# A fused attention and feed-forward kernel: its prologue rebuilt (q loaded first, attention of the first chunk spread over all free PSUM banks, column means of w_out by an fp32 matmul, chunk 1's attention one step earlier and chunk 2's later)

## The chip, the cores and the metric

The kernel runs on one core of a Trainium2 chip. The metric is device time in microseconds (us), from the first to the last instruction of the launch as the runtime counts it; "span" is the same stretch as the profile shows it, about 2 us shorter. Engines are named as in the profile: PE is the matrix engine (PEld its weight loads), DVE the vector engine, ACT the scalar (activation) engine, POOL the GpSimd engine, SP the engine that here issues the output transfers (and three small loads at the start). "Clock" is the share of the full TensorE clock that was granted. Runs are marked fast or slow (over 1.5% above the fastest of the same kernel); only fast ones are compared.

## The reference

```python
def _attn_ref(q, k, v, g_norm):                       # (8 batches, 8 heads, 576, 64)
    kv = np.einsum('bhsd,bhse->bhde', k, v)           # linear attention: no softmax
    out = np.einsum('bhsd,bhde->bhse', q, kv)
    rms = np.sqrt(np.mean(out * out, axis=-1, keepdims=True) + 1e-06)
    return out / rms * g_norm

def _moe_ref(x, w_in, w_out, g_ln):                   # x (4608, 512), w_in (512, 1024)
    h = x @ w_in
    e = np.exp(h - np.max(h, axis=-1, keepdims=True))
    solu = h * (e / (np.sum(e, axis=-1, keepdims=True) + 1e-09))
    mu = np.mean(solu, axis=-1, keepdims=True)
    var = np.mean((solu - mu) ** 2, axis=-1, keepdims=True)
    return ((solu - mu) / np.sqrt(var + 1e-06) * g_ln) @ w_out
```

The attention output, with its heads side by side, is the x of the second function. Everything is float32 at the boundary.

## The kernel before

The 4608 tokens are worked on as nine chunks of 512: one for the first 512 tokens of each batch, and a ninth with the 8 x 64 that remain. A chunk passes through attention (kv, q transposed, o, and the root-mean-square over a head by a matmul with `head_mean`, called s), through eight steps h(c, 0..7) (each four matmuls, an exp on ACT, a product u on DVE, its square usq and a pair sum es on POOL), through statistics (sums, then a few tiny DVE operations), and through the output product.

The layer norm's subtraction of the mean is not done on the tokens. It is folded into the second weight: each row of `w_out * g_ln` has the mean over d_ff of its column taken off, once, in the prologue. So no output matmul may start before that mean is known and the weight is centred:

```python
    def w_out_scale(f, eng):
        eng.tensor_scalar_mul(out=w_out_g[:, f, :], in0=w_out_f[:, f, :], scalar1=g_ln_sb[:, f:f + 1])

    def w_out_mean():
        mean[0] = po.tile([128, d_model], FP32, name="mean_ps", tag="out")
        for f in range(NF):                       # NF = 8; col_mean is 1/1024 everywhere, BF16
            nc.tensor.matmul(mean[0][:, :], col_mean[:, :], w_out_g[:, f, :], start=(f == 0), stop=(f == NF - 1))

    def w_out_center(f):
        nc.vector.scalar_tensor_tensor(
            out=w_out_sb[:, f, :], in0=w_out_f[:, f, :], scalar=g_ln_sb[:, f:f + 1],
            in1=mean[0][:, :], op0=MUL, op1=SUB,
        )
```

The attention of a chunk, per pair of heads p, goes over three PSUM tiles of the pool `pat`:

```python
    def o_mm(c, p):
        ...
        t = pat.tile([128, 512], FP32, name="o_ps", tag="at")
        ... # one matmul kvbd x qT
        osq = work.tile([128, 512], BF16, name="osq")          # work has two buffers of a name
        nc.scalar.activation(out=osq[:, :], in_=t[:, :], func=AF.Square, bias=zero_t[:, :])

    def s_mm(c, p):
        t = pat.tile([128, 512], FP32, name="s_ps", tag="at")
        nc.tensor.matmul(t[:, :], head_mean[:, :], osq_sb.pop((c, p))[:, :], start=True, stop=True)
        ... # lss = Ln(t) and rst = Exp(-0.5 * lss) on ACT
        ... # x_sb = o_ps * g_rep * rst on DVE
```

A plan `at(c, s, fn)` says after which step h(c, s) a piece is issued. In the kernel before, the prologue's plan is:

```python
    at(0, 3, kv_mm, 1); at(0, 3, kv_evac, 1)         # cut: written one per line
    at(0, 4, qT, 1, 0); at(0, 5, qT, 1, 1)
    at(0, 5, o_mm, 1, 0); at(0, 6, s_mm, 1, 0); at(0, 6, o_mm, 1, 1)
    at(0, 7, s_mm, 1, 1); at(0, 7, o_mm, 1, 2); at(0, 7, s_mm, 1, 2); at(0, 7, o_mm, 1, 3); at(0, 7, s_mm, 1, 3)
    for f in range(NF):
        at(0, 4 + f // 4, w_out_scale, f, nc.vector if f % 2 else nc.gpsimd)
    at(0, 6, w_out_mean)
    for f in range(NF):
        at(0, 7, w_out_center, f)
    ... # chunk 2's kv, qT, qT, o: all at (0, 7), behind the eight centrings
    ... # chunks a > 2: kv at (a-2, 4), qT at (a-2, 5) and (a-2, 6), o at (a-2, 7)
    ... # at(c, 0): k, v and both rests (krem, vrem) of batch c+3 are loaded, at(c, 1): q
```

The softmax here doesn't subtract the row's maximum and nothing guards it: scores larger than these inputs give would overflow.

Of the kernel before, what the change touches and what calls it, by code (L numbers as in the profile page):

```python
# [18 lines left out]
def kernel(  # L19
# [47 lines left out]
    krem = [big.tile([128, H, D], BF16, name=f"krem{r}") for r in range(4)]  # L67
    vrem = [big.tile([128, H, D], BF16, name=f"vrem{r}") for r in range(4)]
    qrem = [big.tile([128, H, D], BF16, name=f"qrem{r}") for r in range(4)]
# [10 lines left out]
    def load_rem(ts, src, b):  # L80
        lo = (b % 2) * 64
        nc.gpsimd.dma_start(ts[b // 2][lo:lo + 64, :, :], src[b, :, 512:S, :].rearrange("h s d -> s h d"))

    def load_kv(b):
        load_main(ks, kvl, k, b, "ks")
        load_main(vs, kvl, v, b, "vs")
        load_rem(krem, k, b)
        load_rem(vrem, v, b)
# [3 lines left out]

    load_kv(0)
    load_q(0)
# [19 lines left out]
    col_mean = big.tile([128, 128], BF16, name="col_mean")  # L114
    nc.vector.memset(col_mean, 1.0 / 1024)
# [14 lines left out]
    w_out_g = big.tile([128, NF, d_model], BF16, name="w_out_g")  # L130

    load_kv(1)
    load_q(1)
    for f4 in range(2):
        nc.gpsimd.dma_start(
            w_out_f[:, 4 * f4:4 * f4 + 4, :],
            moe_w_out[f4 * 512:(f4 + 1) * 512, :].rearrange("(n p) d -> p n d", p=128),
        )
    load_kv(2)
    load_q(2)  # L140

# [3 lines left out]
    def kv_mm(b):  # L145
        t = pst.tile([128, NP, 128], FP32, name="kv_ps", tag="st")
        kv_ps[b] = t
        for p in range(NP):
            for j in range(4):
                for hh in range(2):  # L150
                    h = 2 * p + hh
                    nc.tensor.matmul(  # L152
                        t[hh * 64:hh * 64 + 64, p, hh * 64:hh * 64 + 64], ks[b][:, h, j, :], vs[b][:, h, j, :],
                        start=(p == 0 and j == 0), stop=False, skip_group_check=True,
                    )
        lo = (b % 2) * 64
        kr, vr = krem[b // 2], vrem[b // 2]
        for p in range(NP):
            for hh in range(2):
                h = 2 * p + hh  # L160
                nc.tensor.matmul(
                    t[hh * 64:hh * 64 + 64, p, hh * 64:hh * 64 + 64], kr[lo:lo + 64, h, :], vr[lo:lo + 64, h, :],
                    start=False, stop=True, skip_group_check=True,
                )
# [9 lines left out]
    def qT(c, half):  # L174
# [3 lines left out]
        for pp in range(2):  # L178
            p = 2 * half + pp
            for j in range(4):  # L180
                cols = slice(j * 128, (j + 1) * 128)
                if c < B:
                    for hh in range(2):
                        nc.tensor.transpose(t[hh * 64:hh * 64 + 64, pp, cols], qs[c][:, 2 * p + hh, j, :], ident[:, :])  # L184
                else:
                    nc.tensor.transpose(
                        t[:, pp, cols], qrem[j][:, 2 * p:2 * p + 2, :].rearrange("s h d -> s (h d)"), ident[:, :]
                    )
# [4 lines left out]
    def o_mm(c, p):  # L193
        if p == 0:
            x_sb[c] = work.tile([128, NP, 512], BF16, name="x_sb")
        t = pat.tile([128, 512], FP32, name="o_ps", tag="at")
# [7 lines left out]
        osq = work.tile([128, 512], BF16, name="osq")  # L204
# [3 lines left out]
    def s_mm(c, p):  # L208
        t = pat.tile([128, 512], FP32, name="s_ps", tag="at")
# [12 lines left out]
    def h_step(c, f):  # L222
# [4 lines left out]
        t = ph.tile([128, 512], FP32, name="h_ps")  # L227
# [75 lines left out]
    def w_out_scale(f, eng):  # L303
        eng.tensor_scalar_mul(out=w_out_g[:, f, :], in0=w_out_f[:, f, :], scalar1=g_ln_sb[:, f:f + 1])  # L304

    mean = {}

    def w_out_mean():
        mean[0] = po.tile([128, d_model], FP32, name="mean_ps", tag="out")
        for f in range(NF):  # L310
            nc.tensor.matmul(mean[0][:, :], col_mean[:, :], w_out_g[:, f, :], start=(f == 0), stop=(f == NF - 1))  # L311
# [12 lines left out]


    at(0, 3, kv_mm, 1)
    at(0, 3, kv_evac, 1)
    at(0, 4, qT, 1, 0)
    at(0, 5, qT, 1, 1)
    at(0, 5, o_mm, 1, 0)  # L330
    at(0, 6, s_mm, 1, 0)
    at(0, 6, o_mm, 1, 1)
    at(0, 7, s_mm, 1, 1)
    at(0, 7, o_mm, 1, 2)
    at(0, 7, s_mm, 1, 2)
    at(0, 7, o_mm, 1, 3)
    at(0, 7, s_mm, 1, 3)
    for f in range(NF):
        at(0, 4 + f // 4, w_out_scale, f, nc.vector if f % 2 else nc.gpsimd)
    at(0, 6, w_out_mean)  # L340
    for f in range(NF):
        at(0, 7, w_out_center, f)

    for a in range(2, NC):
        if a < B:
            at(a - 2, 4 if a > 2 else 7, kv_mm, a)
            at(a - 2, 4 if a > 2 else 7, kv_evac, a)
        at(a - 2, 5 if a > 2 else 7, qT, a, 0)
        at(a - 2, 6 if a > 2 else 7, qT, a, 1)
        at(a - 2, 7, o_mm, a, 0)  # L350
        for p in range(NP):
            at(a - 1, 2 * p, s_mm, a, p)
            if p + 1 < NP:
                at(a - 1, 2 * p + 1, o_mm, a, p + 1)
    for c in range(NC):
        if c + 3 < B:
            at(c, 0, load_kv, c + 3)
            at(c, 1, load_q, c + 3)
        if c < 4:
            at(c, 2, load_rem, qrem, q, 2 * c)  # L360
            at(c, 2, load_rem, qrem, q, 2 * c + 1)
# [10 lines left out]

    kv_mm(0)
    kv_evac(0)
    qT(0, 0)
    qT(0, 1)
    o_mm(0, 0)
    for p in range(NP):
        if p + 1 < NP:
            o_mm(0, p + 1)  # L380
        s_mm(0, p)
# [38 lines left out]
```

## Time and profile before

| | before |
|---|---|
| device time, median of 3 runs (range) | 262.22 us (260.02 to 262.8) |
| span of the profiled run, mean clock | 258.9 us, 0.929 |
| busy PE / DVE / ACT / POOL | 76% / 56% / 47% / 64% |
| chunk interval in the middle of the run (sums to sums) | 21.9 us |
| first h group closed to first h group of chunk 1 | 29.4 to 76.8 us, 47.4 us |

First the page's row of 40 slices, each 6.5 us wide: the busy tenths of PE and the granted clock in tenths.

```profile
PE   0244793244259899979979979998997998997972
PEclk9999999555559999999999999999999999999997
```

PE is full from about slice 13 on and, but for two slices, thin before it, and the clock is at half for five slices. The loss is in the first 80 us. The next fence is the view by windows of the same trace (columns: window, length, busy us with the number of instructions on PE, PEld, DVE, ACT, POOL, then clock, mean DMA share, GB/s): chunk 0's stretch and one chunk of the middle.

```profile
29.40:76.80 47.40, 23.08 (x190) 10.08 (x190) 24.43 (x32) 13.33 (x20) 25.54 (x23) 0.66 0.71 106
98.90:120.80 21.90, 20.24 (x174) 9.83 (x172) 14.74 (x27) 13.32 (x23) 18.54 (x19) 1.00 0.88 133
```

In the middle PE is busy 20.24 of 21.9 us: it paces the kernel. In the first window it is busy less than half. The waits view says on what (columns: engine and line, what it waited for, total us, times, longest):

```profile
PE mean_ps L311 <- POOL w_out_g L304: 12.4, 4, 8.6
```

And the timeline shows the two serial stretches (columns: start, duration, engine, line, operation, output and inputs, count; in brackets the idle time before and what ended it). First the scaled copy `w_out_g` and the mean that waits for it:

```profile
41.87 5.24 DVE L304 TENSOR_SCALAR w_out_g<-w_out_f,g_ln_sb 128x512 bf16<-128x512 f32 x2
47.99 3.12 POOL L304 TENSOR_SCALAR w_out_g<-w_out_f,g_ln_sb 128x512 bf16<-128x512 f32 x2
49.62 1.01 PE L311 MATMUL mean_ps<-w_out_g,col_mean 128*128 128x512 bf16 x2 [8.59 <-POOL w_out_g L304]
...
56.47 1.01 PE L311 MATMUL mean_ps<-w_out_g,col_mean 128*128 128x512 bf16 x2 [0.53 <-POOL w_out_g L304]
```

Then what stands between the mean and chunk 1:

```profile
67.33 5.34 DVE L314 SCALAR_TENSOR_TENSOR w_out_sb<-w_out_f,g_ln_sb,mean_ps 128x512 bf16<-128x512 f32 x8
72.60 0.85 DVE L170 CAST kvbd<-kv_ps 64x256 bf16<-64x256 f32 x2
73.59 1.07 PE L184 MATMUL qT_ps<-ident,qs 128*64 128x128 bf16 x16 [7.09 <-DVE kvbd L170]
...
76.84 1.91 PE L229 MATMUL h_ps<-x_sb,w_in_sb 128*128 128x512 bf16 x4
```

PE waits 7.09 us for an evacuation of chunk 2's kv that stands in DVE's queue behind all eight centrings, although PE's next h group belongs to chunk 1 and needs none of it.

### The profile page before, as it was taken

Reading aid. Unit: us, or ns where it says so; the run is one execution under the profiler, and the core shown is the slowest. Engines: PE = TensorE matmul, PEld = TensorE weight load, DVE = VectorE, ACT = ScalarE, POOL = GpSimd, SP = SyncE. Lnnn points to the kernel's source line nnn. Section 1 sums busy time; section 2 is a strip of 40 time slices with the busy share of each in tenths; the row PEclk is TensorE's granted clock in tenths of the full one; section 3 lists DMA queues with packets and bytes.
Section 4 is the critical chain, followed back from the end, with each engine's and each line's share of the span. In section 5 each row is a group of like instructions: output and inputs, shape, how many; then the busy total and the mean of one; then the engine's idle time right before and its main releaser. Section 6 shows DMA issues by size and latency. Waiting matters only on the chain.

```text
span 258.9 us, 3911 instructions
## 1 busy us (share of the span) xinstructions
PE 197.2 (76%) x1528; PEld 93.5 (36%) x1528; DVE 145.9 (56%) x258; ACT 122.2 (47%) x199; POOL 166.8 (64%) x170
## 2 busy tenths in 40 slices
PE   0244793244259899979979979998997998997972
PEld 0230241011134544444534445454453544443330
DVE  1532369403754568586576756857656666655442
ACT  1017635007205757366655565746666666623200
POOL 8543469983005976995997797565585584695800
PEclk9999999555559999999999999999999999999997
DMA  6999999900001992992597299201111121122215
GB/s 68 162 204 191 342 216 194 183 3 0 3 0 16 184 169 82 120 205 82 88 187 134 81 160 187 83 2 41 71 54 41 43 81 40 44 81 81 81 33 133
DMA packets 45698, 27.00 MB, mean 104 GB/s; under 512 B 14960, under 2 KB 40560, under 8 KB 45680
## 3 DMA queue, kind: packets, MB, share of 16 engines
q0 software_dynamic: 39232, 17.30, 51.2%
q1 hardware_dynamic: 6448, 9.44, 11.1%
q8 instruction: 12, 0.20, 0.3%
q14 instruction: 6, 0.05, 0.1%
HBM read 32.51 MB, written 9.44 MB: 162 GB/s over the span
## 4 chain that ended last, share of the span: by engine, by line
PE 48%; ACT 18%; DVE 15%; POOL 9%; issue 4%; DMA 4%; POOLq 0%; ACTq 0%; DVEq 0%
PE h_ps L229 18%; PE out_ps L286 16%; ACT rst L214 5%; ACT lss L212 5%; PE qT_ps L184 4%; DVE x_sb L215 4%; ACT e_sb L236 4%; DMA qs<-in_q_dram 4%; PE sum_ps L251 4%; POOL usq_sb L238 3%; PE s_ps L210 2%; POOL w_out_g L304 2%; DVE kvbd L170 2%; DVE w_out_sb L314 2%; POOL es_sb L240 2%
## 5 line engine op out<-in xcount | busy, mean ns | idle before, releaser
L238 POOL TENSOR_TENSOR usq_sb<-u_sb 128x512 bf16<-128x512 bf16 x72 | 75.8, 1054 | 64.3 <-DVE u_sb L237 64.2
L236 ACT ACTIVATE e_sb<-h_ps,zero_t 128x512 f32<-128x512 f32 x72 | 49.2, 683 | 73.9 <-PE h_ps L229 71.5
L229 PE MATMUL h_ps<-x_sb,w_in_sb 128*128 128x512 bf16 x288 | 78.7, 399 | 0.9 <-DVE x_sb L215 0.8
L237 DVE TENSOR_TENSOR u_sb<-h_ps,e_sb 128x512 bf16<-128x512 f32 x72 | 49.4, 686 | 50.8 <-ACT e_sb L236 50.5
L286 PE MATMUL out_ps<-w_out_sb,u_sb 128*128 128x512 bf16 x288 | 73.2, 379 | 3.7 <-DVE ob L294 3.7
L240 POOL TENSOR_TENSOR es_sb<-e_sb 128x512 bf16<-128x512 f32 x36 | 45.9, 1274 | 0.0
L215 DVE SCALAR_TENSOR_TENSOR x_sb<-o_ps,g_rep,rst 128x512 bf16<-128x512 f32 x36 | 27.0, 750 | 29.3 <-ACT rst L214 29.3
L229 PEld LDWEIGHTS <-w_in_sb 128*128 128x128 bf16 x288 | 28.5, 104 | 39.0 <-issue 12.0
L286 PEld LDWEIGHTS <-u_sb 128*128 128x128 bf16 x288 | 26.5, 98 | 37.3 <-issue 8.6
L206 ACT ACTIVATE osq<-o_ps,zero_t 128x512 bf16<-128x512 f32 x36 | 24.3, 679 | 27.2 <-PE o_ps L199 27.2
L294 DVE TENSOR_SCALAR ob<-out_ps,rstd 128x512 f32<-128x512 f32 x36 | 26.7, 744 | 3.2 <-PE out_ps L286 2.3
L214 ACT ACTIVATE rst<-lss,zero_t 128x512 f32<-128x512 f32 x36 | 26.0, 722 | 1.2
L212 ACT ACTIVATE lss<-s_ps,eps_t 128x512 f32<-128x512 f32 x36 | 24.6, 684 | 3.1 <-PE s_ps L210 3.1
L210 PE MATMUL s_ps<-osq,head_mean 128*128 128x512 bf16 x36 | 15.2, 422 | 14.0 <-ACT osq L206 11.3
L184 PE MATMUL qT_ps<-ident,qs 128*64 128x128 bf16 x256 | 11.9, 244 | 12.6 <-DVE kvbd L170 8.9
L184 PEld LDWEIGHTS <-qs 128*64 128x64 bf16 x256 | 9.4, 124 | 18.5 <-issue 16.2
L189 DVE COPY qT_sb<-qT_ps 128x1024 bf16<-128x1024 bf16 x18 | 12.3, 682 | 5.9 <-PE qT_ps L184 5.9
L152 PE MATMUL kv_ps<-vs,ks 128*64 128x64 bf16 x256 | 6.3, 208 | 11.5 <-DMA vs<-in_v_dram 11.5
L199 PE MATMUL o_ps<-qT_sb,kvbd 128*128 128x512 bf16 x32 | 13.6, 430 | 1.6 <-ACT lss L212 1.6
L152 PEld LDWEIGHTS <-ks 128*64 128x64 bf16 x256 | 5.5, 123 | 23.2 <-issue 9.6
L311 PE MATMUL mean_ps<-w_out_g,col_mean 128*128 128x512 bf16 x8 | 4.0, 608 | 12.4 <-POOL w_out_g L304 12.4
L275 ACT ACTIVATE lv<-vare,zero_t 128x4 f32<-128x4 f32 x9 | 2.7, 297 | 20.9 <-DVE vare L271 20.9
(51 smaller groups left out, 146.3 us busy)
## 6 DMA issues: line engine op xcount, KB each, us to landing
out_dram<-ob SPq DMA_DIRECT2D x32, 256.0 KB, 2.3
ks<-in_k_dram POOLq DMA_DIRECT2D x8, 512.0 KB, 6.7
vs<-in_v_dram POOLq DMA_DIRECT2D x8, 512.0 KB, 8.7
qs<-in_q_dram POOLq DMA_DIRECT2D x8, 512.0 KB, 9.6
w_out_f<-in_moe_w_out_dram POOLq DMA_DIRECT2D x2, 1024.0 KB, 16.4
w_in_sb<-in_moe_w_in_dram POOLq DMA_DIRECT2D x2, 512.0 KB, 13.0
out_dram<-ob SPq DMA_DIRECT2D x8, 128.0 KB, 2.3
krem<-in_k_dram POOLq DMA_DIRECT2D x8, 64.0 KB, 8.2
```

Source lines behind the costliest of these rows:

```text
L184: nc.tensor.transpose(t[hh * 64:hh * 64 + 64, pp, cols], qs[c][:, 2 * p + hh, j, :], ident[:, :])
L206: nc.scalar.activation(out=osq[:, :], in_=t[:, :], func=AF.Square, bias=zero_t[:, :])
L212: nc.scalar.activation(out=lss[:, :], in_=t[:, :], func=AF.Ln, bias=eps_t[:, :])
L214: nc.scalar.activation(out=rst[:, :], in_=lss[:, :], func=AF.Exp, scale=-0.5, bias=zero_t[:, :])
L215: nc.vector.scalar_tensor_tensor(out=x_sb[c][:, p, :], in0=o_ps.pop((c, p))[:, :], scalar=g_rep[:, :], in1=rst[:, :], op0=MUL, op1=MUL)
L229: nc.tensor.matmul(t[:, :], w_in_sb[:, dt, f * 128:(f + 1) * 128], x_sb[c][:, dt, :], start=(dt == 0), stop=(dt == NP - 1),)
L236: nc.scalar.activation(out=e[:, f % 2, :], in_=t[:, :], func=AF.Exp, bias=zero_t[:, :])
L237: nc.vector.tensor_tensor(out=u_sb[c][:, f, :], in0=t[:, :], in1=e[:, f % 2, :], op=MUL)
L238: nc.gpsimd.tensor_tensor(out=usq_sb[c][:, f, :], in0=u_sb[c][:, f, :], in1=u_sb[c][:, f, :], op=MUL)
L240: nc.gpsimd.tensor_tensor(out=es_sb[c][:, f // 2, :], in0=e[:, 0, :], in1=e[:, 1, :], op=ADD)
L286: nc.tensor.matmul(t[:, :], u_sb[c][:, f, m * 128:(m + 1) * 128], w_out_sb[:, f, :], start=(f == 0), stop=(f == NF - 1),)
L294: nc.vector.tensor_scalar_mul(out=ob[:, :], in0=t[:, :], scalar1=rstd_sb[c][:, m:m + 1])
```

## The change

Its intent is to take these serial stretches out. The mean is computed directly from the loaded fp32 `w_out_f`, with `g_ln/1024` as the stationary operand, so the scaled copy and its wait go. q of batch 0 is loaded first so that its transposes run while k and v land; chunk 0's four o and four s products get a PSUM tile each. Chunk 2's attention moves out of the end of chunk 0 into chunk 1; chunk 1's attention, the mean and half of the centrings are issued one step earlier. The loads of the rests of k and v move one step later than those of k and v, and the four tiles of each kind of rest become one. The diff, cut to its core:

```diff
-    krem = [big.tile([128, H, D], BF16, name=f"krem{r}") for r in range(4)]      # vrem, qrem likewise
+    krem = big.tile([128, 4, H, D], BF16, name="krem")
     ...
+    load_q(0)
     load_kv(0)
-    load_q(0)
+    load_rem(krem, k, 0); load_rem(vrem, v, 0)        # load_kv no longer loads the rests
     ...
-    w_out_g = big.tile([128, NF, d_model], BF16, name="w_out_g")
+    g_mean = big.tile([128, NF, 128], FP32, name="g_mean")
+    nc.vector.tensor_scalar_mul(
+        out=g_mean[:, :, :], in0=g_ln_sb[:, :, None].to_broadcast([128, NF, 128]), scalar1=1.0 / d_ff
+    )
     ...                                               # w_out_f: one load of 2 MB instead of two of 1 MB
-        osq = work.tile([128, 512], BF16, name="osq")
+        osq = epool.tile([128, 512], BF16, name="osq")            # four buffers instead of two
     ...
-            nc.tensor.matmul(mean[0][:, :], col_mean[:, :], w_out_g[:, f, :], start=(f == 0), stop=(f == NF - 1))
+            nc.tensor.matmul(mean[0][:, :], g_mean[:, f, :], w_out_f[:, f, :], start=(f == 0), stop=(f == NF - 1))
     ...
+    at(0, 2, kv_mm, 1)              # chunk 1's attention: each piece one step earlier
+    ...
+    at(0, 5, w_out_mean)
+    for f in range(NF):
+        at(0, 6 + f // 4, w_out_center, f)
+    at(1, 0, kv_mm, 2)
+    at(1, 0, kv_evac, 2)
+    at(1, 0, qT, 2, 0)
+    at(1, 2, qT, 2, 1)
+    at(1, 2, o_mm, 2, 0)
+    for p in range(NP):
+        at(1, 3 + p, s_mm, 2, p)
+        if p + 1 < NP:
+            at(1, 3 + p, o_mm, 2, p + 1)
     ...
+    for b in range(2, B):
+        c, s = (0, 2) if b == 2 else (max(b - 3, 0), 6) if b == 3 else (b - 3, 0)
+        at(c, s, load_kv, b)
+        at(c, s + 1, load_rem, krem, k, b)
+        at(c, s + 1, load_rem, vrem, v, b)
+        at(c, s + 2 if s < 6 else s + 1, load_q, b)
     ...
+    qT(0, 0)
+    qT(0, 1)
     kv_mm(0)
     kv_evac(0)
-    qT(0, 0)
-    qT(0, 1)
-    o_mm(0, 0)
     for p in range(NP):
-        if p + 1 < NP:
-            o_mm(0, p + 1)
-        s_mm(0, p)
+        o_mm(0, p, *((pat, "at") if p < 3 else (po, "out")))
+    for p in range(NP):
+        s_mm(0, p, *((ph, "h") if p < 3 else (po, "out")))
```

## The prediction

> **What bounds it now.** The stage view: from 77 to 229 us a steady state, about 21.9 us per chunk with 20.3 us of PE busy at clock 1.00, so PE paces it. The end (229 to 259) is untouched. The loss is the start. In the timeline the first h group gets its last input at 29.4 us and the first h group of chunk 1 starts at 76.8: chunk 0 takes 47.5 us, not 22.
>
> - The waits view: "PE mean_ps <- POOL w_out_g" 12.4 us (longest 8.6). w_out_g is made on POOL and DVE between usq, es and DMA issues; PE has 3.6 us of work from 42 to 57.
> - The clock falls to 0.50 until 77 (the slices' PEclk row).
> - 57 to 77 runs serially: three s/o steps with two osq buffers, eight w_out_sb (5.3 us), then kv, qT (1.07 us per group) and o of chunk 2, all ahead of h(1,0).
>
> **What the change does.**
>
> 1. Chunk 0's attention. The q transposes (2 x 1.07 us, two 0.69 us copies) run while k and v land. The last input still lands near 15 us, so o starts at 17.7 us as before. But the osq run ahead: ACT's 12 activations of 0.68-0.72 us take 8.4 us instead of 10.0. h(0,0) closes at about 27.6 us, gain 1.8.
> 2. w_out_g disappears (13.6 us of DVE and POOL) with PE's wait. In its place are 8 fp32 matmuls of 512 columns. The Trainium skill, FP8 and Floating Point Precision, "TensorE Precision Notes", says true fp32 takes four passes; the trace shows only that 36 fp32 st_ps products are 72 PE records. Estimate: four passes at the warm 0.216 us (four h matmuls in 0.86) is 0.86 each, 6.9 us in all; 13.8 if cold. w_out_f lands at about 34.2 us as now; PE reaches the mean at 38.5 and leaves at 45.4, instead of 57.3: gain about 12.
> 3. Then h6, h7, the last three s/o steps and the first four w_out_sb in DVE's order. x(1,3), so h(1,0), comes at about 54.8 us: 22 us earlier.
> 4. Given back: kv, qT and o of chunk 2 move into chunk 1: 0.96 + 1.28 + 0.2 us of PE warm, more when cold, plus waits for evacuations. PE is thin from 48 to 55 us, so the clock should have fallen and need some 5 us of dense work (29.4 to 34.7 before). The skill's TensorE page, "The HAM clock gate", gives 3.4 us windows; the trace agrees roughly. Together about 4.5 us.
> 5. One DVE op for g_mean (estimate 1.1 us) before 12 us, off the path. Split rem loads and the single w_out_f load: no gain in steady state.
>
> Net 22 - 4.5 = 17.5 us, nearly all on the critical path: 262.2 - 17.5 gives 244.5 us. Range 239 to 250. Chances: faster 0.96, same 0.03, slower 0.01.
>
> **What would show it.** No w_out_g group; a mean_ps group of 16 records, about 7 us busy, no idle before it; h(0,0) closed at 27-28 us; h(1,0) at 53-57; the clock at 0.5 only around 50-60 us instead of 45-77; steady chunks again 21.9 us; from h(1,0) to h(2,0) 25-27 us instead of 21.9.
>
> **What would make it wrong.** The mean at half clock (7 us worse); passes other than four; w_out_f later as one transfer; q ahead of v making v late; chunk 1's crowding (two chunks' attention, one PSUM buffer for kv, qT and stats) costing more than 4.5 us; or a clock low through chunk 1.

## More of the kernel before

The tiny operations of a chunk's statistics, which matter later:

```python
        nc.vector.tensor_copy(st[:, :, :], st_ps[:, :, :])
        nc.vector.tensor_tensor(out=sq[:, :, :], in0=st[:, :, 1:3], in1=st[:, :, 1:3], op=MUL)
        nc.vector.tensor_tensor(out=var[:, :], in0=st[:, :, 0], in1=sq[:, :, 0], op=SUB)
        nc.vector.scalar_tensor_tensor(out=vare[:, :], in0=sq[:, :, 1], scalar=1e-6 * d_ff * d_ff,
                                       in1=var[:, :], op0=MUL, op1=ADD)
        ... # lv = Ln(vare), rstd = Exp(-0.5 * lv) on ACT
```

## The result and the profile after

| | before | after |
|---|---|---|
| device time, median (range) of 4 runs | 262.33 us (260.02 to 262.8) | 243.24 us (242.32 to 243.54) |
| ratio of fast runs, 95% interval | | 0.928 (0.922 to 0.934) |
| span and clock of the profiled run | 258.9 us, 0.929 | 241.3 us, 0.958 |
| exp of h(1,0) starts on ACT | 78.85 us | 52.35 us |
| first sums of the statistics start (chunk 0) | 81.74 us | 61.24 us |
| third sums start (chunk 2) | 124.81 us | 106.80 us |
| last sums start (chunk 8), then to the end | 244.53 us, 14.4 us | 225.18 us, 16.1 us |

A ratio here is the mean time of one kernel's fast runs over that of the other's of the same rounds, so it is not quite the ratio of the medians quoted. All kernels in this document gave correct results.

The slices of the changed kernel, each 6.0 us wide:

```profile
PE   0164899557989997998999899899979989979971
PEclk9998599965999999999999999999999999999979
```

The half-clock stretch between chunks 0 and 1 has shrunk from five slices (the 8th to the 12th) to two (the 9th and 10th). The 5 in slice 5 is chunk 0's first dense h matmuls; the row of the kernel before shows 9 there, although 13 such matmuls took 5.41 us from 29.36 on, 0.42 us each, as long as at half clock. So close to the start of the trace the clock row is not to be trusted, and the durations decide. The window from the first closed h group to the close of h(1,0), in the same columns as above:

```profile
25.80:52.20 26.40, 21.28 (x131) 8.89 (x130) 13.51 (x22) 13.10 (x20) 18.94 (x20) 0.89 1.03 182
```

From the closing of h(0,0) to the closing of h(1,0) it is now 26.4 us, where it was 49.3 (29.4 to the end of the group that starts at 76.84 and takes 1.91). The timeline of the prologue:

```profile
11.03 0.69 DVE L130 TENSOR_SCALAR g_mean<-g_ln_sb 128x1024 f32<-128x1024 f32 x1
11.64 0.68 DVE L187 COPY qT_sb<-qT_ps 128x1024 bf16<-128x1024 bf16 x1
...
14.22 1.07 PE L150 MATMUL kv_ps<-vs,ks 128*64 128x64 bf16 x32 [0.78 <-DVE qT_sb L187]
...
16.60 1.89 PE L197 MATMUL o_ps<-qT_sb,kvbd 128*128 128x512 bf16 x4 [0.96 <-DVE kvbd L168]
17.24 2.42 ACT L204 ACTIVATE osq<-o_ps,zero_t 128x512 bf16<-128x512 f32 x4 [15.22 <-PE o_ps L197]
...
25.82 4.00 PE L227 MATMUL h_ps<-x_sb,w_in_sb 128*128 128x512 bf16 x9 [0.75 <-DVE x_sb L213]
...
35.92 7.03 PE L306 MATMUL mean_ps<-w_out_f,g_mean 128*128 128x512 f32 x16
42.78 1.03 PE L227 MATMUL h_ps<-x_sb,w_in_sb 128*128 128x512 bf16 x4
```

The four o products run without a pause, their squares follow on ACT without a pause, and the mean has no idle time before it: 16 records (each fp32 product shows as two), 35.92 until the next group at 42.78. From the first product to the start of the next group it is 6.86 us. The first lines show that chunk 0's kv waited for DVE: v had landed at 13.5 us (issued at 3.19, 10.3 us to landing), but kv started at 14.22, when DVE had made `g_mean` and both copies of the transposed q.

What follows is the place where some of the gain is given back, around the start of chunk 1:

```profile
51.53 2.71 DVE L309 SCALAR_TENSOR_TENSOR w_out_sb<-w_out_f,g_ln_sb,mean_ps 128x512 bf16<-128x512 f32 x4
51.67 0.58 PE L227 MATMUL h_ps<-x_sb,w_in_sb 128*128 128x512 bf16 x1 [0.49 <-DVE x_sb L213]
52.18 1.06 PE L150 MATMUL kv_ps<-vs,ks 128*64 128x64 bf16 x32
...
54.76 0.85 DVE L168 CAST kvbd<-kv_ps 64x256 bf16<-64x256 f32 x2
...
55.76 1.06 PE L182 MATMUL qT_ps<-ident,qs 128*64 128x128 bf16 x16 [2.16 <-DVE kvbd L168]
56.75 1.89 PE L284 MATMUL out_ps<-w_out_sb,u_sb 128*128 128x512 bf16 x4
...
58.43 1.91 PE L227 MATMUL h_ps<-x_sb,w_in_sb 128*128 128x512 bf16 x4
...
61.24 0.62 PE L249 MATMUL sum_ps<-usq_sb,stat_sel 128*32 128x512 bf16 x8
```

kv of chunk 2 is issued right behind h(1,0); its evacuation stands in DVE's queue behind the last four centrings, and PE waits 2.16 us for it. The clock is at half: groups of four matmuls take 1.89 and 1.91 us, against 1.03 us at full clock (42.78).

Two things further on differ that no part of the prologue explains. The first is in the statistics of the chunks that load (POOL, DVE and PE, before and then after; `sq` starts 5.25 us after the chunk's own sums in both). The lines before belong to chunk 2's sums, those after to chunk 3's; chunk 2's own `sq` in the changed kernel also takes 0.17 us (at 112.04):

```profile
129.55 1.30 POOL L240 TENSOR_TENSOR es_sb<-e_sb 128x512 bf16<-128x512 f32 x1
130.06 0.82 DVE L267 TENSOR_TENSOR sq<-st 128x8 f32<-128x8 f32 x1
133.14 0.38 PE L210 MATMUL s_ps<-osq,head_mean 128*128 128x512 bf16 x1 [1.41 <-ACT osq L206]
```

```profile
131.37 1.28 POOL L238 TENSOR_TENSOR es_sb<-e_sb 128x512 bf16<-128x512 f32 x1
133.25 0.17 DVE L265 TENSOR_TENSOR sq<-st 128x8 f32<-128x8 f32 x1
135.68 0.38 PE L208 MATMUL s_ps<-osq,head_mean 128*128 128x512 bf16 x1 [0.75 <-ACT osq L204]
```

Before, `sq` took 0.82 us and ended just as `es` ended on POOL (130.06 + 0.82 = 130.88; 129.55 + 1.30 = 130.85). After, `es` is over when `sq` starts, `sq` takes 0.17 us, and PE's next wait is 0.66 us shorter: the last of the tiny operations is awaited by `lv` on ACT, and the `osq` that PE waits for stands behind `lv` in ACT's queue. Of the three intervals from sums to sums that took 21.85 to 21.87 us before, two take 21.20 and 21.21 us now; the third (chunk 2) stays at 21.97 us, because there another tiny operation, `vare`, meets a POOL instruction (shown at e8). `es` comes 1.4 us earlier, counted from the sums, because POOL issues the two rests of k and v (0.72 and 0.71 us in the trace before) after it and no longer ahead of it.

The second is the tail. The last 16 matmuls, before and then after, with the same wait of 1.42 us ahead of them:

```profile
250.38 3.61 PE L286 MATMUL out_ps<-w_out_sb,u_sb 128*128 128x512 bf16 x16 [1.42 <-DVE ob L294]
```

```profile
231.02 5.30 PE L284 MATMUL out_ps<-w_out_sb,u_sb 128*128 128x512 bf16 x16 [1.42 <-DVE ob L292]
```

In the profiled run of the changed kernel the clock was 0.51 from 231 to 234 us. That gave back 1.7 us.

In sum, by the profiled runs: h(1,0) is 26.5 us earlier; 20.5 us of that are left at the first sums and 18.0 at the third; 1.3 us come back by the last sums (244.53 - 225.18 = 19.35); 1.75 us go in the tail (14.37 to 16.12); 17.6 us remain (258.9 - 241.3).

### The profile page after: what moved, and what is told of

It is laid out like the page before. It is cut to its first block, busy times and chain, and to the rows that moved or that the text cites. A ratio compares the mean times of both kernels' runs of the same rounds, so it can differ in the third digit from the quotient of the medians.

```text
span 241.3 us, 3920 instructions
## 1 busy us (share of the span) xinstructions
PE 199.5 (83%) x1536; PEld 95.1 (39%) x1536; DVE 138.0 (57%) x254; ACT 121.5 (50%) x199; POOL 159.4 (66%) x165
## 4 chain that ended last, share of the span: by engine, by line
PE 53%; ACT 19%; DVE 16%; issue 6%; POOL 4%; POOLq 0%; ACTq 0%
PE out_ps L284 18%; PE h_ps L227 18%; ACT rst L212 5%; ACT lss L210 5%; ACT e_sb L234 5%; PE sum_ps L249 4%; DVE x_sb L213 4%; PE qT_ps L182 4%; PE mean_ps L306 3%; DVE kvbd L168 2%; ACT osq L204 2%; DVE u_sb L235 2%; PE s_ps L208 2%; PE o_ps L197 2%; DVE ob L292 1%
## 5 line engine op out<-in xcount | busy, mean ns | idle before, releaser
L236 POOL TENSOR_TENSOR usq_sb<-u_sb 128x512 bf16<-128x512 bf16 x72 | 75.0, 1043 | 62.4 <-DVE u_sb L235 62.1
L284 PE MATMUL out_ps<-w_out_sb,u_sb 128*128 128x512 bf16 x288 | 75.9, 391 | 3.7 <-DVE ob L292 3.7
L227 PEld LDWEIGHTS <-w_in_sb 128*128 128x128 bf16 x288 | 27.9, 102 | 42.8 <-issue 15.4
L284 PEld LDWEIGHTS <-u_sb 128*128 128x128 bf16 x288 | 27.1, 100 | 38.9 <-issue 11.9
L208 PE MATMUL s_ps<-osq,head_mean 128*128 128x512 bf16 x36 | 13.7, 392 | 10.7 <-ACT osq L204 9.7
L197 PE MATMUL o_ps<-qT_sb,kvbd 128*128 128x512 bf16 x32 | 12.5, 411 | 1.0 <-DVE kvbd L168 1.0
L254 DVE COPY sums<-sum_ps 128x512 f32<-128x512 f32 x9 | 6.2, 691 | 8.4 <-PE sum_ps L249 8.4
L261 PEld LDWEIGHTS st_ps<-stat_pick,sums 128*128 128x128 f32 x72 | 9.3, 191 | 2.2 <-DVE qT_sb L187 0.9
```

Source lines behind the costliest of these rows:

```text
L227: nc.tensor.matmul(t[:, :], w_in_sb[:, dt, f * 128:(f + 1) * 128], x_sb[c][:, dt, :], start=(dt == 0), stop=(dt == NP - 1),)
L236: nc.gpsimd.tensor_tensor(out=usq_sb[c][:, f, :], in0=u_sb[c][:, f, :], in1=u_sb[c][:, f, :], op=MUL)
L284: nc.tensor.matmul(t[:, :], u_sb[c][:, f, m * 128:(m + 1) * 128], w_out_sb[:, f, :], start=(f == 0), stop=(f == NF - 1),)
```

## The experiments

My theory, A: the gain is the mean (no scaled copy, no wait) and the order of chunk 2 behind it, with a small part from chunk 0's attention; part is given back at the start of chunk 1 for chunk 2's pieces and a low clock; and the steady chunks are shorter because POOL and DVE no longer meet. Rivals: B, chunk 0's attention (q first, more PSUM tiles) carries much of the gain; C, the steady chunks are shorter because `osq` has four buffers; D, what chunk 1 gives back is a matter of where chunk 2's pieces stand, not of the clock. For the kernels below, "after" is the changed kernel; medians of the kernel before were between 261.67 and 261.83 us in these calls. The changed kernel was not run again in them, so a difference of about 1 us between two of its variants is not clear of the noise by the medians alone. The traces have a spread of their own: in e9 and the changed kernel PE's timeline agrees up to 29.75 us, but then a kv product takes 0.241 us in e9 (half clock) and 0.196 in the changed kernel, and the mean starts 0.8 us later; e12, whose edit is at the end only, has its first sums 0.7 us earlier. So a shift of the first sums by less than about 1 us can be the moment at which the clock rises in chunk 0.

| run | built on | median us (range) | ratio to before (95%) | first sums, us | span, us |
|---|---|---|---|---|---|
| before | | 262.33 (260.02 to 262.8) | 1 | 81.74 | 258.9 |
| after | | 243.24 (242.32 to 243.54) | 0.928 (0.922 to 0.934) | 61.24 | 241.3 |
| e1 mean alone | before | 250.72 (249.71 to 251.96) | 0.958 (0.952 to 0.963) | 70.57 | 247.7 |
| e2 k, v ahead of q | after | 244.24 (243.71 to 244.44) | 0.932 (0.929 to 0.936) | 61.64 | 241.6 |
| e3 three tiles, interleaved | after | 245.16 (244.62 to 245.67) | 0.935 (0.932 to 0.939) | 63.74 | 243.8 |
| e4 rests with k and v | after | 250.17 (245.32 to 250.64), 3 of 4 slow | none | 61.69 | 248.8 (slow) |
| e5 two osq buffers | after | 243.52 (242.88 to 244.14) | 0.931 (0.926 to 0.936) | 61.76 | 241.8 |
| e6 chunk 2 early | after | 242.22 (242.03 to 243.02) | 0.927 (0.923 to 0.931) | 64.86 | 240.3 |
| e7 mean in BF16 | after | 237.57 (236.48 to 238.46) | 0.908 (0.904 to 0.913) | 56.25 | 234.6 |
| e8 statistics from PSUM | after | 240.32 (239.95 to 241.16) | 0.919 (0.916 to 0.923) | 61.04 | 238.1 |
| e9 unread matmuls, start | after | 240.6 (239.1 to 241.99) | 0.920 (0.915 to 0.925) | 60.11 | 240.1 |
| e10 combination | after | 234.9 (234.03 to 234.97) | 0.897 (0.892 to 0.903) | 55.87 | 233.1 |
| e11 combination, warm | e10 | 233.26 (232.0 to 234.46) | 0.890 (0.885 to 0.896) | 53.22 | 230.1 |
| e12 unread matmuls, tail | after | 241.77 (240.76 to 242.58) | 0.923 (0.919 to 0.928) | 60.53 | 238.9 |

### e1: the mean alone, in the kernel before

```diff
-    w_out_g = big.tile([128, NF, d_model], BF16, name="w_out_g")
+    g_mean = big.tile([128, NF, 128], FP32, name="g_mean")
+    nc.vector.tensor_scalar_mul(
+        out=g_mean[:, :, :], in0=g_ln_sb[:, :, None].to_broadcast([128, NF, 128]), scalar1=1.0 / d_ff
+    )
-            nc.tensor.matmul(mean[0][:, :], col_mean[:, :], w_out_g[:, f, :], start=(f == 0), stop=(f == NF - 1))
+            nc.tensor.matmul(mean[0][:, :], g_mean[:, f, :], w_out_f[:, f, :], start=(f == 0), stop=(f == NF - 1))
-    for f in range(NF):
-        at(0, 4 + f // 4, w_out_scale, f, nc.vector if f % 2 else nc.gpsimd)
```

> The kernel before with only the mean changed (fp32 matmuls on w_out_f, no w_out_g; old load order, old schedule). Theory A (w_out_g's wait was the largest single loss, the rest adds to it): PE enters the mean at about 41.5 us and leaves at about 48.5 instead of 57.3, and with no long idle stretch the clock stays up for part of what follows: 249 to 253 us. Rival B (the new schedule is what pays; after the mean the old serial stretch and the half clock remain): above 256 us.

Measured: 250.72 us. The mean runs from 40.41 to 47.27 us instead of ending at 57.3, and the first sums come 11.2 us earlier (81.74 - 70.57); the span is 11.2 us shorter. The timeline of e1:

```profile
40.41 7.03 PE L309 MATMUL mean_ps<-w_out_f,g_mean 128*128 128x512 f32 x16
...
62.28 1.06 PE L185 MATMUL qT_ps<-ident,qs 128*64 128x128 bf16 x16 [7.24 <-DVE kvbd L171]
```

The mean by itself is 11.2 of the 17.6 us, about six tenths. PE's wait for chunk 2's kv behind the eight centrings is untouched here (7.24 us); with the new order of the changed kernel it is 2.16. Theory A holds on this point.

### e2 and e3: the two halves of the new chunk 0

e2 puts k and v ahead of q again, in the loads and on PE:

```diff
-    load_q(0)
     load_kv(0)
     load_rem(krem, k, 0)
     load_rem(vrem, v, 0)
+    load_q(0)
     ...
-    qT(0, 0)
-    qT(0, 1)
     kv_mm(0)
     kv_evac(0)
+    qT(0, 0)
+    qT(0, 1)
```

> The changed kernel with k and v loaded before q and the q transposes after kv, as before; the rest new. Theory A: the first o matmul starts at about 17.9 us instead of 16.6 and all that follows moves by as much: +1 to +1.5 us. Rival B (the loads for the mean, w_out_f landing at 34.7 us, pace chunk 0, so an earlier start is absorbed): within 0.3 us.

e3 gives chunk 0's o and s only the three tiles of `pat`, interleaved as before:

```diff
+    o_mm(0, 0)
     for p in range(NP):
-        o_mm(0, p, *((pat, "at") if p < 3 else (po, "out")))
-    for p in range(NP):
-        s_mm(0, p, *((ph, "h") if p < 3 else (po, "out")))
+        if p + 1 < NP:
+            o_mm(0, p + 1)
+        s_mm(0, p)
```

> The changed kernel with chunk 0's o and s back in three PSUM banks and in the old order; q still first. Theory A: the 12 activations take about 10.0 us instead of 8.3, h(0,0) closes 1.7 to 2.2 us later, and the time grows by as much. Rival B (absorbed by the wait for w_out_f before the mean): within 0.3 us.

Measured: with e2 the first h group closes from 26.81 instead of 25.82 us, but the mean starts only 0.6 us and the first sums only 0.4 us later; the median is 1.0 us longer. With e3 the first h group closes from 28.05, the mean starts at 38.28, the first sums come 2.5 us later, and the median is 1.9 us longer. Together the new chunk 0 is worth about 3 us if the two simply add, which no run tested. Rival B falls: most of the gain lies elsewhere. The one microsecond of q first is shown at the first h group; how much of it reaches the end is not, since 0.4 us at the first sums is within the spread named above and the ratio's interval overlaps that of the changed kernel (e3's overlaps too, but its 2.5 us in the trace are beyond the spread).

### e4: the rests loaded with k and v again

```diff
         at(c, s, load_kv, b)
-        at(c, s + 1, load_rem, krem, k, b)
-        at(c, s + 1, load_rem, vrem, v, b)
+        at(c, s, load_rem, krem, k, b)
+        at(c, s, load_rem, vrem, v, b)
```

> The changed kernel with the rem loads of k and v issued in the same step as k and v, as before. Theory A (the shorter steady chunks come from POOL's es no longer overlapping DVE's two-input sq of the statistics): sq takes about 0.82 us again in the chunks that load, s waits about 1.4 us for osq there, the chunks take 21.85 us instead of 21.2, and the whole is 1.3 to 2.5 us longer. Rival B (four osq buffers instead of two shorten them): no change, sq stays at 0.17 us.

Measured: one fast run of 245.32 us, 2.1 above the median of the changed kernel; three runs of 250.15 to 250.64 us count as slow, and the profile is of one of them. Since the profile is of a slow run, only who waits for whom is read from it, not its time (POOL and DVE, from the timeline):

```profile
113.46 1.30 POOL L238 TENSOR_TENSOR es_sb<-e_sb 128x512 bf16<-128x512 f32 x1
113.99 0.80 DVE L265 TENSOR_TENSOR sq<-st 128x8 f32<-128x8 f32 x1
114.68 1.06 POOL L236 TENSOR_TENSOR usq_sb<-u_sb 128x512 bf16<-128x512 bf16 x1
114.83 0.95 DVE L267 TENSOR_TENSOR var<-st,sq 128x4 f32<-128x4 f32 x1
```

With the two load issues ahead of it on POOL, `es` meets `sq` again, and the following `usq` now meets `var` as well: two tiny operations in a row end with the POOL instruction they overlap. That agrees with A. The size (2.1 us for three or four loading chunks) rests on a single fast run and is not settled. In this profile PE waits 2.16 us after these operations and the clock is then at half for about 3.5 us. The slow profile's loss lies in just the three intervals with stretched pairs (23.47, 23.98 and 23.97 us, where the changed kernel has 21.97, 21.20 and 21.21); the interval before them and those behind them are as in the changed kernel. Whether the slow mark is a state of the chip or comes of this edit, these runs don't tell.

### e5: osq in two buffers

```diff
-        osq = epool.tile([128, 512], BF16, name="osq")
+        osq = work.tile([128, 512], BF16, name="osq")
```

> The changed kernel with two osq buffers, as before, instead of four. Theory A (the buffers matter only in chunk 0, where four osq run ahead, and hardly there): steady chunks stay at 21.2 us, sq stays at 0.17 us, and the whole changes by under 0.7 us. Rival B (the four buffers shorten the steady chunks): chunks of 21.85 us and 1.3 to 2 us more.

Measured: 243.52 us; the steady chunks are 21.2 us and `sq` takes 0.17 us, as in the changed kernel. Rival C falls. That chunk 0 with two buffers is hardly slower (first sums 0.5 us later) suggests that it was the PSUM tiles, more than these buffers, that mattered there.

### e6: chunk 2's attention at the end of chunk 0 again

```diff
-    at(1, 0, kv_mm, 2)
-    at(1, 0, kv_evac, 2)
-    at(1, 0, qT, 2, 0)
-    at(1, 2, qT, 2, 1)
-    at(1, 2, o_mm, 2, 0)
+    at(0, 7, kv_mm, 2)
+    at(0, 7, kv_evac, 2)
+    at(0, 7, qT, 2, 0)
+    at(0, 7, qT, 2, 1)
+    at(0, 7, o_mm, 2, 0)
     for p in range(NP):
-        at(1, 3 + p, s_mm, 2, p)
+        at(1, 2 * p, s_mm, 2, p)
         if p + 1 < NP:
-            at(1, 3 + p, o_mm, 2, p + 1)
+            at(1, 2 * p + 1, o_mm, 2, p + 1)
```

> The changed kernel with kv, qT and o of chunk 2 back in chunk 0's last step, ahead of h(1,0), and its s steps spread over chunk 1 as before. Theory A (in the old place they stand in series behind the w_out_sb operations on DVE; in the new place they cost 2.4 us more in chunk 1, which takes 23.6 instead of 21.2): h(1,0) starts some 6 us later, the first sums about 3 us later, chunk 1 takes 21.2 us again, net +0.5 to +2 us. Rival B (the move gains all of the 6 us): +4 us or more.

Measured: h(1,0) comes 9.1 us later by its exp (61.44; some 6 were expected) and the first sums 3.6 us later (64.86), but the next interval is 21.43 instead of 23.59 us and the one after it 21.20 instead of 21.97; at the eighth sums the kernel is only 0.7 us behind (210.08 to 209.39). Then its last 16 matmuls run at full clock, so the median is 242.22 us, 1.0 below that of the changed kernel, with overlapping intervals. By the median the expected loss missed; up to the tail it is there (0.7 us). The later place of chunk 2 moves the work from ahead of the first sums to behind them. Of what e6 catches up, 0.77 us is not a matter of place: in its second interval `vare` does not meet POOL's `usq` and takes 0.16 us, where the changed kernel's takes 0.93. Without that the later place would win about 1.5 us (an estimate, 0.7 + 0.77), still less than the tail differs from run to run.

### e7: the mean in BF16

```diff
-    w_out_f = big.tile([128, NF, d_model], FP32, name="w_out_f")
+    w_out_f = big.tile([128, NF, d_model], BF16, name="w_out_f")
-    g_mean = big.tile([128, NF, 128], FP32, name="g_mean")
+    g_mean = big.tile([128, NF, 128], BF16, name="g_mean")
```

> The changed kernel with w_out cast to bf16 by its load and g_mean in bf16, so that the mean is 8 single-pass matmuls; the centring then starts from the rounded weights (the error may grow a little). Theory A (the mean's 6.9 us stand on the critical path, and the four passes are what they cost): the mean takes about 1.75 us, everything after comes 4.5 to 5.2 us earlier, 238 to 239 us. Rival B (ACT's chain of chunk 1's attention or the landing of w_out paces that stretch): under 2 us gained.

Measured: 237.57 us, 5.7 below the changed kernel's median. One of the eight products is missing from the trace:

```profile
36.42 1.89 PE L306 MATMUL mean_ps<-w_out_f,g_mean 128*128 128x512 bf16 x7
38.15 1.03 PE L227 MATMUL h_ps<-x_sb,w_in_sb 128*128 128x512 bf16 x4
```

The mean takes 1.73 us (36.42 to 38.15), or 0.216 per product, where fp32 took 6.86, or 0.858: a factor of 4.0. The Trainium skill, "FP8 and Floating Point Precision", section "TensorE Precision Notes", says that true fp32 takes four passes through the array; this agrees. The first sums come 5.0 us earlier, so nearly all of the 5.1 us was on the critical path. The rest of the difference of the profiles (241.3 to 234.6) is the tail, which ran at full clock here. The weights that the output products use were BF16 in any case (`w_out_sb`); here they are centred from a BF16 copy.

### e8: the statistics read one operand from PSUM

```diff
-        st_ps = pst.tile([128, 4, 3], FP32, name="st_ps", tag="st")
+        st_ps = pst.tile([128, 4, 8], FP32, name="st_ps", tag="st")
     ...
-        nc.vector.tensor_tensor(out=sq[:, :, :], in0=st[:, :, 1:3], in1=st[:, :, 1:3], op=MUL)
-        var = work.tile([128, 4], FP32, name="var")
-        nc.vector.tensor_tensor(out=var[:, :], in0=st[:, :, 0], in1=sq[:, :, 0], op=SUB)
+        nc.vector.tensor_tensor(out=sq[:, :, :], in0=st_ps[:, :, 1:3], in1=st[:, :, 1:3], op=MUL)
+        var = st_ps[:, :, 4]
+        nc.vector.tensor_tensor(out=var, in0=st_ps[:, :, 0], in1=sq[:, :, 0], op=SUB)
```

> The changed kernel with sq, var and vare each reading one operand from PSUM and one from SBUF, so that no small DVE operation has two SBUF inputs. Theory A (those operations wait out a POOL operation only when both of their inputs are in SBUF): none of them is above 0.3 us any more; the two stretched ones (vare 0.93 us in chunk 2, sq 0.74 us in the last stage) lose their 0.6 to 0.8 us each, 0.6 to 1.4 us less in all. Rival B (the stretch has another cause, such as the DMA issues): they stay stretched and the time is the same.

Measured: 240.32 us, 2.9 below the changed kernel. The same place in chunk 2's interval, in the changed kernel and then in e8 (timeline, POOL and DVE):

```profile
90.31 1.06 POOL L236 TENSOR_TENSOR usq_sb<-u_sb 128x512 bf16<-128x512 bf16 x1
90.47 0.93 DVE L269 SCALAR_TENSOR_TENSOR vare<-sq,var 128x4 f32<-128x4 f32 x1
```

```profile
90.11 1.06 POOL L236 TENSOR_TENSOR usq_sb<-u_sb 128x512 bf16<-128x512 bf16 x1
90.29 0.16 DVE L269 SCALAR_TENSOR_TENSOR vare<-sq,st_ps 128x4 f32<-128x4 f32 x1
```

In both, the tiny DVE operation starts inside the POOL instruction. With two SBUF inputs it lasts until POOL is done (90.47 + 0.93 = 91.40; 90.31 + 1.06 = 91.37); with one input in PSUM it takes 0.16 us and ends well inside it. This is the cleanest run for the mechanism: same overlap, other operand. POOL's load issues, the rival in the expectation, do not stretch: in the changed kernel `var`, with two SBUF inputs, ran at 133.45 inside the issue of `vrem` (133.31 to 134.00) and took 0.16 us. The Trainium skill, "SBUF — State Buffer", section "Who interferes with whom", says that a DVE instruction with two SBUF inputs contends with a GpSimd instruction that reads SBUF, that this contention is an exclusive lock, and that one with at most one SBUF input, outside the 2-port modes, does not contend. Chunk 2's interval falls from 21.97 to 21.20 us and the last from 15.79 to 15.22, 1.3 us in all; of the rest of the profile's difference 1.7 us are the tail, which ran at full clock here (3.61 us), and 0.2 us were there at the first sums. I don't count these parts for e8.

### e9: unread matmuls to keep the clock up at the start of chunk 1

```diff
+    def warm(n):
+        if not warm_t:
+            warm_t[0] = po.tile([128, d_model], FP32, name="warm_ps", tag="out")
+        for _ in range(n):
+            nc.tensor.matmul(warm_t[0][:, :], ident[:, :], w_in_sb[:, 0, 0:512], start=True, stop=True)
     ...                           # 4 and 7 of them among the last s/o steps of (0, 7), 8 behind kv at (1, 0)
```

> The changed kernel with 19 matmuls whose result is never read, put into PE's idle time around the start of chunk 1 (4 and 7 between the s steps at 44 to 49 us, 8 while kv of chunk 2 is copied at 54 us), so that the clock does not fall. Theory A (the half clock from about 49 to 60 us is a cost of its own): kv, qT, out and h of that stretch run at 0.7, 0.64 and 0.86 us per group instead of 1.06, 1.06 and 1.7 to 1.9, and the first sums come 2 to 3.5 us earlier, at about 58 us; the whole gains as much. Rival B (ACT and DVE pace that stretch, the clock only fills waits): under 1 us gained.

Measured: the groups behind them, in the timeline of e9:

```profile
56.85 0.64 PE L182 MATMUL qT_ps<-ident,qs 128*64 128x128 bf16 x16
57.42 1.04 PE L284 MATMUL out_ps<-w_out_sb,u_sb 128*128 128x512 bf16 x4
58.29 1.03 PE L227 MATMUL h_ps<-x_sb,w_in_sb 128*128 128x512 bf16 x4
```

They take 0.64, 1.04 and 1.03 us instead of 1.06, 1.89 and 1.91. The first sums come at 60.11, 1.1 us earlier; counted from h(0,6), which here happened to start 0.8 us later (43.61 instead of 42.78), 2.0 us earlier, the lower end of what was expected. The 0.8 us is the clock's later rise in chunk 0, named above. kv itself, at 53.01, still took 1.06 us, so the half clock was not wholly gone. So the low clock is at least about 2 us of what chunk 1 gives back. The six runs of this kernel fall into two groups, 239.1 to 239.6 and 241.6 to 242.0, and its profile is of the second, with a slow tail (5.24 us for the last 16 matmuls); no profile of the first group was kept, so the difference is not explained. Rival D holds only for a part: place (e6) and clock (e9) both count.

### e12: unread matmuls in the tail

```diff
+    def warm_tail(n):
+        t = ph.tile([128, 512], FP32, name="warm_ps", tag="h")
+        for _ in range(n):
+            nc.tensor.matmul(t[:, :], ident[:, :], w_in_sb[:, 0, 0:512], start=True, stop=True)
     ...
+        if c == B:
+            at(c + 1, 3, warm_tail, 7)
         at(c + 1, 3, out_evac, c, 0)
```

> The changed kernel with 7 unread matmuls between the second last chunk-8 output group and the wait for its evacuation. Theory A (the changed kernel gave back up to 1.7 us at its end because the clock falls there in most executions, which in the kernel before it did not): the last 16 output matmuls take 3.6 us instead of 5.3 and the runs lie at 241.3 to 242.5 us, 0.8 to 1.7 below the changed kernel. Rival B (the tail is paced by DVE and the DMAs): no change.

Measured: 241.77 us over six runs, 1.5 below the changed kernel's median, with overlapping intervals. In the timeline of e12 the gap of 1.42 us is filled and the last 16 matmuls take 3.61 instead of 5.30 us:

```profile
228.78 1.67 PE L318 MATMUL warm_ps<-w_in_sb,ident 128*128 128x512 bf16 x7
230.36 3.61 PE L284 MATMUL out_ps<-w_out_sb,u_sb 128*128 128x512 bf16 x16
```

The tail's loss is the clock. What decides whether it drops without the filling is not settled: with the same gap of 1.42 us in the same place, the profiled runs of before, e1, e6, e7 and e8 kept their clock, and those of the changed kernel, e2, e3, e5 and e9 lost it. The Trainium skill, "TensorE: Matmul & The Clock Gate", section "What's actually happening", says that activity is judged in free-running windows of about 3.4 us that do not start with the kernel. A drop that depends on where the window falls would fit; no run here shows the windows.

### e10 and e11: a version that beats both

e10 joins e7 and e8, puts the last four centrings behind chunk 2's kv and first q transposes, and spreads the last chunk's outputs over four PSUM tiles, so that PE need not wait for an evacuation. Beside the diffs of e7 and e8:

```diff
-    for f in range(NF):
-        at(0, 6 + f // 4, w_out_center, f)
+    for f in range(4):
+        at(0, 6, w_out_center, f)
     ...
     at(1, 0, qT, 2, 0)
+    for f in range(4, NF):
+        at(1, 0, w_out_center, f)
     ...
-            o_acc[m] = po.tile([128, d_model], FP32, name="out_ps", tag="out")
+            pool, tag = (ph, "h") if c == NC - 1 and m >= 2 else (po, "out")
+            o_acc[m] = pool.tile([128, d_model], FP32, name="out_ps", tag=tag)
     ...                           # and the last chunk's pieces listed in that order
```

> A version meant to beat both: the bf16 load and single-pass mean, the statistics read from PSUM, the first four centrings one step earlier and the last four after chunk 2's qT, and the last chunk's four output groups in four PSUM banks (two of them h's, free by then), so that PE need not wait for the evacuation of the first two. Expected from the parts: 5.7 for the mean, 1.3 for the statistics, about 1 for the centrings, and 3 to 4 at the end, where the last 16 matmuls now start only after rstd: 231 to 234 us.

Measured: 234.9 us, a shade above what was expected. The automatic verdict of this run was left at unclear; its interval (0.892 to 0.903) lies wholly below 1. The first sums are only 0.4 us earlier than in e7, so moving the four centrings won little. The timeline of its tail shows what ends the kernel now (SPq is SP's queue of transfer issues):

```profile
222.65 3.61 PE L285 MATMUL out_ps<-w_out_sb,u_sb 128*128 128x512 bf16 x16
...
225.07 4.99 SPq L300 DMA_DIRECT2D out_dram<-ob  x8
```

PE is done by about 226.3 us, but the eight output transfers are issued one after another by SP, 0.62 us each, until 230.06. e11 therefore lets ACT evacuate and issue half of them, and adds 16 unread matmuls as in e9:

```diff
+        if c == B and m % 2:
+            nc.scalar.activation(out=ob[:, :], in_=t[:, :], func=AF.Identity, scale=rstd_sb[c][:, m:m + 1], bias=zero_t[:, :])
+        else:
             nc.vector.tensor_scalar_mul(out=ob[:, :], in0=t[:, :], scalar1=rstd_sb[c][:, m:m + 1])
     ...
-                nc.sync.dma_start(out[t0:t0 + 64, :], ob[bb * 64:(bb + 1) * 64, :])
+                eng = nc.scalar if m % 2 else nc.sync
+                eng.dma_start(out[t0:t0 + 64, :], ob[bb * 64:(bb + 1) * 64, :])
     ...                           # warm(4) and warm(7) at (0, 7), warm(5) at (1, 0)
```

> The combined version with, in addition, 16 unread matmuls that keep the clock up around the start of chunk 1 (they write the bank that the first output group then overwrites), and with the last chunk's evacuations and output DMAs split over DVE with SP and ACT with its own queue. Expected: first sums at about 54 us instead of 55.9; the eight last issues, 5 us in a row on SP in the combined version, in about 3 us; 230 to 232 us in all against 234.9. If issue is not what ends the kernel, or the clock does not matter there, one of the two gains is missing.

Measured: 233.26 us, the best here, 1.3 us above the range that was expected; the first sums come at 53.22. SP's four issues take 2.90 us and end at 225.33, ACT's last two end at 225.92, where e10's ended 5 us after they began. The gap from the last sums to the end is 14.27 us (230.1 - 215.83), against 14.63 in e10 (233.1 - 218.47): the split tail won 0.4 us, the unread matmuls 2.6 us at the first sums. Its interval overlaps that of e10, which ran in another call, so that e11 is the faster of the two is likely, not shown. Both are faster than the changed kernel by 3% or more.

## Why the prediction was right

The total, 244.5 us, was within 1.3 us of the median and inside the range. Point by point:

1. **Chunk 0's attention.** Predicted: o starts at 17.7, ACT's twelve activations take 8.4 us, the first h group closes at 27.6, gain 1.8. Measured: 16.60, 7.7 us from the start of the first to the end of the last (17.24 to 24.98), 25.82. "The last input still lands near 15 us, so o starts at 17.7 us as before" was wrong: o started 1.3 us earlier (17.91 before). q, which was the last to land (15.03), is now the first; v landed at 13.5 and its rest at 14.3, and what stands between the landings and o is kv and its evacuation (14.22 to 16.60) and no longer two rounds of q transposes with their copies (15.06 to 17.91). Nor was `g_mean` "off the path", as point 5 of the prediction has it: kv started 0.7 us after v had landed, because it waited for q's copies on DVE, and the first of these stood directly behind `g_mean` (0.69 us, predicted 1.1). By these numbers a `g_mean` made later would have given some 0.6 us (an estimate; no run tested it). e3 and e2 put the values of the two halves at 1.9 and 1.0 us.
2. **The mean.** Predicted: start 38.5, end 45.4, 6.9 us. Measured: 35.92 to 42.78, 6.86 us of products. e1 showed that it is worth 11.2 us alone (predicted: about 12), and e7 that the four passes of fp32 cost 5.0 us of it.
3. **Chunk 1 starts 22 us earlier.** Measured: 26.5 us. The step that failed is its time of arrival: "h(1,0), comes at about 54.8 us"; the last group of it ran at 51.67. The mean started 2.6 us earlier than predicted (1.8 of it is chunk 0's: 25.82 for 27.6), the way from the mean's end to that group was 0.5 us shorter than predicted, and the group itself was no longer one block of 1.91 us: three of its four matmuls were done while the last x was still being made, and the last took 0.58. These three make up 4.4 of the 4.5 us.
4. **"Together about 4.5 us" given back.** Mis-sized: it was 8.5 us (26.5 less 18.0), of which 6.0 before the first sums and 2.5 in the two intervals behind them. Inside it are a wait of 2.16 us for the evacuation of kv behind four centrings, which the prediction named only as "plus waits for evacuations", and about 2 us of low clock (e9). "From h(1,0) to h(2,0) 25-27 us" was too short for the same reason: from exp to exp it is 29.6 us (52.35 to 81.97; before, 78.85 to 100.11, 21.3). The wait by itself was worth little: e10 more than halved it (1.07 us), and its first sums came only 0.4 us earlier than e7's.
5. **"no gain in steady state" for the split loads.** Wrong. Two chunks are about 0.66 us shorter each, 1.3 us in all (19.35 - 18.0); a third would be, but for the stretched `vare`. The order of POOL's load issues decided whether `es` met the tiny DVE operations; e8 showed the mechanism, e5 excluded the buffers, and e4 pointed the same way with one fast run. The prediction looked at the transfers' bytes, not at the time that their issue takes on POOL.
6. **The tail** was said to be untouched. It lost 1.75 us in the profiled run to a clock drop (e12 filled it), but not in every profiled run.

So the net was right because errors cancelled, which was luck: 22 - 4.5 = 17.5 as predicted, and 26.5 - 8.5 + 1.3 - 1.7 = 17.6 in the profiled runs. By the medians the gain is 19.1 us (262.33 - 243.24); the profiled runs were 261.15 and 243.18. The direction and the main term (the mean off POOL and DVE, off the critical path) were right for the reason given; the two terms of points 3 and 4 were each about 4 us off in opposite directions.

What stays open: why the tail's clock falls in some runs and not in others, the two groups of e9, and the size of e4. One part of the change no run took out: chunk 1's attention, the mean and half of the centrings one step earlier. If the parts simply add, it is the rest of the 9.3 us by which the changed kernel's first sums are ahead of e1's: 2.9 us are e2's and e3's, 3.6 e6's, and some 2.8 are left for it (an estimate, with the spread of about 1 us named above). The single tile for each kind of rest and the single load of `w_out_f` were not tested apart either.

## What to carry to other kernels

Follow a constant of the prologue, such as a column mean, back to its inputs: an fp32 matmul straight from the loaded weights was four times as long as a BF16 one and still 11 us better than preparing a BF16 copy on engines that had other work, and a BF16 load was better still. When work is moved out of a prologue, size what it does at its new place, in the queue of each engine that evacuates it and at the clock that is granted there, since more came back here (8.5 us) than the moved matmuls alone would take. Look for tiny operations whose duration varies from chunk to chunk: here 0.17 us became 0.82 us when it started inside one of POOL's arithmetic instructions (a load issue on POOL did not do it), and an operand in PSUM, or POOL's load issues in another order, cured it.

## What the Trainium skill lacked or had wrong

- "TensorE: Matmul & The Clock Gate" gives, as a working rule, no PE gaps over about 3.4 us. Here the clock fell with much shorter gaps: at the start of chunk 1 the longest gap since chunk 0's dense work was 1.89 us, with PE busy 0.89 us in the 3 us from 47 to 50, and in the tail after one gap of 1.42 us. The page does describe short idles between groups that make the clock oscillate, for a kernel that cycles through PSUM, but gives no measure for them; the runs here show no threshold either.
- The same page's figure, a ramp of under 1% of a typical span, is for the warm-up at the start and does not cover later drops. Here one half-clock stretch cost about 2 us at the start of chunk 1 (e9) and another 1.5 to 1.7 us in the tail (e12), together 1.5% of 241.3 us. Unread matmuls took most of the first and all of the second away; the page's windows alone do not tell when they are needed, since the same 1.42 us gap kept the full clock before and in e8.
- "SBUF — State Buffer" has the rule on two SBUF inputs right, but does not say what it costs tiny operations on a critical path: 0.17 us became 0.82 us, worth 0.65 us per chunk, and two operations in a row could be caught by two successive POOL instructions (0.80 and 0.95 us in e4). That an operand left in PSUM avoids it follows from the page; e8 measured it (0.93 us to 0.16 us).
- "DMA: Bandwidth & Descriptors", section "Issuing engines are not separate DMA queues", calls the issue time saved by a second issuing engine usually small relative to the transfer. At the end of a kernel it is visible: eight issues in a row took 4.99 us on one queue (e10), and 2.90 us where half of them went to a second (e11), although only 0.4 us of it showed in the last stage.
- "DMA: Bandwidth & Descriptors" counts the making of a load's descriptors on GpSimd as latency of the load; no page that I read states what it costs that engine's other work: here 0.7 to 0.95 us each on POOL, enough that their order moved `es` by 1.4 us and changed the length of a chunk.
